# A top-32 attention with a two-expert layer on one core: third replacements, low parts and products moved between engines, row sends and check passes re-ordered

## The chip, the cores and the metric

The kernel runs on one core of a Trainium2 chip. The core's engines are TensorE (PE, with its weight loads as PEld), VectorE (DVE), ScalarE (ACT), GpSimd (POOL) and SyncE (SP), which issues DMAs. The metric is device time in microseconds (us), the median of several runs of the same program.

## The reference, cut to what matters

Every query keeps only its 32 largest scores. The attention's output is then the input of a layer of eight experts, of which each token uses two.

```python
# attention: B, H, S, D = 4, 8, 576, 64; top_k = 32
scores = scale * np.matmul(q, k.transpose(0, 1, 3, 2))
kth = np.partition(scores, -top_k, axis=-1)[..., -top_k:-top_k + 1]
scores = np.where(scores >= kth, scores, -1000000000.0)
attn = softmax(scores)
x = np.matmul(attn, v)            # 2304 rows of 512
# experts: E, F = 8, 1024
noisy = x @ w_gate + np.log1p(np.exp(x @ w_noise)) * noise
top2, top2_w = the two largest of noisy, softmax over the two
out[mask] += top2_w[mask, k, None] * (np.maximum(x[mask] @ w1[e], 0.0) @ w2[e])
```

## The kernel before, in words

The attention is cut into 144 tiles of 128 query rows, 36 for each of the four batches, `attend(j)` and `finish(j)`. For one tile the PE makes scores (L577 in batch 0, L581 later), ACT copies one half of them out (`s`, L589), and DVE folds the two halves into `cat` (maxima, then minima, L612). DVE then takes four rounds of eight maxima (L616); between rounds it overwrites the eight it has found (`drop8`, MATCH_REPLACE8, L621, over 208, 240 and 288 columns). The third replacement can be done instead by a sign on ACT (`side`, L627) and a product on GpSimd (`drop`, L630); `DROPS` gives, for each batch, in how many tenths of the tiles that is so. ACT makes the exponentials `es` (L644), a mask `mk` is made of the 32nd value, either on DVE (`mask`, L648) or as a sign on ACT (L682, after a small `below`, L678; `SIGNS` gives the tenths), and `es` is multiplied by the mask (`weigh`, L693). PE turns the product (L708, L712), ACT copies it (L716, L720), and PE multiplies by the values (L761, L768, L770).

In batches 1 to 3 the scores are made of rounded operands. ACT rounds keys and queries (`hi`, L515), and two subtractions, `low_k` (L519) and `low_q` (L522), give what the rounding left out. Each of them can go to GpSimd or to DVE.

When a batch's 36 tiles are done, `gate` and `route` choose the experts, and ten indirect DMAs from GpSimd (`scatter`, L1044, each with a small memset, L1043) send the batch's rows into per-expert buffers `xg` in DRAM. The experts run in three groups. Group 0 takes rows of batch 0 in plain fp32 (L1229, L1239, L1274) and needs the sends of batch 0; group 1 needs those up to batch 2; group 2 those of all four. Groups 1 and 2 split the weights into a rounded part (`wh`, ACT, L1112) and a rest (`wl`, L1116, on GpSimd or DVE), and multiply three times (L1200 to L1202 upward, L1282 to L1284 downward). Between them ACT and DVE split each hidden tile into `hh` (L1206) and `hl` (L1210), and each input tile into `xh` (L1170) and `xl` (L1173).

The order of all this is written by a planner, `Plan.order`, at build time: every piece has an engine, an assumed duration, dependencies and a priority, and each engine's list is then fixed. A piece with an `alt` may go to a second engine; a number (`LOWK`, `WEIGHS`, `BIAS`, `NORM`, `BELOW`, `LOWS`) shifts that choice in each batch. On the chip every engine works down its own list in that order and waits where an operand is not there. Where PE has nothing to do ahead of group 0, the planner puts in `filler` multiplies of a dummy tile (L542), in a number that `FILL` and `KEEP` set.

At the end the kernel checks that its shortcuts held (`flags`, L1006 to L1020, all on DVE, reading `over`, `under`, `left` and `apart`); if a flag is set, a slow general path follows.

## Time and profile before

| what | us |
|---|---|
| median of 3 runs | 998.77 |
| lowest and highest of them | 997.01, 1000.16 |
| the profiled execution's own time | 1007.95 |
| its span, first to last instruction | 1006.2 |

The profile is of one execution, so stretches of it are read against 1007.95 us, not against the median. Windows are counted from the span's start. By the trace batch 0's attention runs to about 150 us, group 0 from 192 to 522 us, group 1 from 520 us, the last tile's product is turned at 730 us, and from about 786 us on only group 2 is left; the last multiply of group 2 ends at 989 us. Busy shares of PE count the whole length of each multiply, and multiplies overlap. The granted clock is TensorE's, as a share of its upper level; its two levels are 1.2 and 2.4 GHz.

### The profile page before, as it was taken

What the parts mean: (1) busy time and instruction counts of PE and PEld (TensorE: products, weight loads), DVE (VectorE), ACT (ScalarE), POOL (GpSimd) and SP (SyncE); (2) the same over time, 40 slices, a digit from 0 to 9 for tenths busy, and PEclk for the clock granted to TensorE, in tenths of its full rate; (3) what the DMA queues carried; (4) which work ended last, traced back from release to release, by engine and by line L of the source; (5) the groups of instructions that cost most, each with busy time, mean ns of one, the idle gap of its engine ahead of it and who ended that gap; (6) DMA issues with size and microseconds to landing.
All of it is one profiled execution on the core that took longest, in us unless ns stands there. A gap on an engine that the chain in (4) does not pass through costs nothing.

```text
span 1006.2 us, 18439 instructions
## 1 busy us (share of the span) xinstructions
PE 940.1 (93%) x6160; PEld 788.6 (78%) x6176; DVE 695.3 (69%) x2190; ACT 680.0 (68%) x1533; POOL 742.4 (74%) x926
## 2 busy tenths in 40 slices
PE   9999998899999899999699999899978999999993
PEld 4777776787887677888489988799867888999892
DVE  6999998799999799999783578877784222222220
ACT  5888885688987478887476668577635555555550
POOL 4676677355657666677689889687858899999991
PEclk9999999799998999999999999999979999999997
DMA  9477222157366664566667677354556877776741
GB/s 281 162 259 258 49 70 93 28 155 214 125 175 175 234 172 113 154 188 149 217 231 220 168 199 191 96 159 137 137 158 206 245 215 232 233 226 211 230 126 25
DMA packets 109385, 173.92 MB, mean 173 GB/s; under 512 B 7648, under 2 KB 60896, under 8 KB 109280
## 3 DMA queue, kind: packets, MB, share of 16 engines
q1 hardware_dynamic: 100576, 152.42, 48.8%
q0 software_dynamic: 8704, 20.22, 9.7%
q8 instruction: 51, 0.84, 0.3%
q14 instruction: 54, 0.44, 0.1%
HBM read 136.34 MB, written 36.27 MB: 172 GB/s over the span
## 4 chain that ended last, share of the span: by engine, by line
PE 61%; DVE 11%; POOL 10%; ACT 7%; issue 5%; DMA 2%; another core or an unknown queue 1%; SPq 0%; POOLq 0%; DVEq 0%; ACTq 0%
PE bank L768 7%; PE hps L1200 4%; POOL wl L1116 4%; PE hps L1202 4%; PE hps L1201 4%; PE pp L708 4%; PE bk L577 4%; PE bk L581 4%; PE bk L1274 3%; PE bk L1284 3%; PE bk L1282 3%; DVE t L616 3%; PE bk L1283 3%; PE hps L1229 3%; PE hps L542 3%
## 5 line engine op out<-in xcount | busy, mean ns | idle before, releaser
L1116 POOL TENSOR_TENSOR wl<-wr,wh 128x1024 fp32r<-128x1024 f32 x118 | 292.6, 2717 | 26.6 <-ACT wh L1112 14.0
L616 DVE MAX8 t<-cat 128x8 f32<-128x288 f32 (+3 forms) x576 | 268.1, 490 | 9.4 <-POOL cat L630 6.7
L693 POOL TENSOR_TENSOR es<-es,mk 128x576 f32<-128x576 f32 x140 | 187.2, 1341 | 94.2 <-ACT mk L682 74.9
L1112 ACT ACTIVATE wh<-wr 128x1024 fp32r<-128x1024 f32 x128 | 133.7, 1056 | 51.1 <-PE bk L1284 25.4
L1210 DVE SCALAR_TENSOR_TENSOR hl<-hps,hh 128x256 fp32r<-128x256 f32 x128 | 53.8, 421 | 155.6 <-ACT hh L1206 152.8
L621 DVE MATCH_REPLACE8 cat<-t,cat 128x208 f32<-128x208 f32 (+2 forms) x408 | 159.9, 394 | 0.0
L1200 PE MATMUL hps<-xh,wh 128*128 128x256 f32 x512 | 149.9, 293 | 2.2 <-DVE hl L1210 2.2
L612 DVE TENSOR_TENSOR cat<-bk,s 128x288 f32<-128x288 f32 x288 | 125.5, 444 | 33.7 <-ACT s L589 33.5
L1202 PE MATMUL hps<-xh,wl 128*128 128x256 f32 x512 | 145.9, 285 | 0.5 <-POOL wl L1116 0.5
L1201 PE MATMUL hps<-xl,wh 128*128 128x256 f32 x512 | 145.8, 285 | 0.0
L768 PEld LDWEIGHTS bank<-vt,pt 128*128 128x128 f32 x1024 | 124.1, 196 | 15.1 <-ACT p L720 10.4
L768 PE MATMUL bank<-vt,pt 128*128 128x65 f32 x1024 | 126.3, 278 | 7.1 <-ACT p L720 7.0
L589 ACT ACTIVATE s<-bk 128x288 f32<-128x288 f32 x288 | 111.5, 416 | 31.8 <-PE bk L581 19.4
L644 ACT ACTIVATE es<-s,nb 128x576 f32<-128x576 f32 x144 | 111.7, 777 | 4.6 <-POOL nb L638 2.6
L716 ACT ACTIVATE pt<-pp 128x512 f32<-128x512 f32 x144 | 86.3, 599 | 33.8 <-PE pp L708 27.2
L1200 PEld LDWEIGHTS hps<-xh,wh 128*128 128x128 f32 x512 | 98.5, 192 | 4.6 <-DVE hl L1210 2.5
L1201 PEld LDWEIGHTS hps<-xl,wh 128*128 128x128 f32 x512 | 98.5, 192 | 2.0
L1202 PEld LDWEIGHTS hps<-xh,wl 128*128 128x128 f32 x512 | 98.3, 192 | 0.7 <-POOL wl L1116 0.7
L1206 ACT ACTIVATE hh<-hps 128x256 fp32r<-128x256 f32 x128 | 48.8, 381 | 70.6 <-PE hps L1202 66.2
L708 PE MATMUL pp<-ident,es 128*128 128x128 f32 x576 | 89.5, 278 | 7.1 <-POOL es L693 4.0
L682 ACT ACTIVATE mk<-s,under 128x576 bf16<-128x576 f32 x107 | 83.0, 780 | 16.4 <-POOL under L678 11.8
L581 PE MATMUL bk<-hi 128*128 128x288 f32 x240 | 90.0, 384 | 3.0 <-DVE cat L612 1.6
(155 smaller groups left out, 2048.0 us busy)
## 6 DMA issues: line engine op xcount, KB each, us to landing
wr<-in_w_dram SPq DMA_DIRECT2D x192, 512.0 KB, 4.7
raw<-in_qk_dram SPq DMA_DIRECT2D x48, 320.0 KB, 8.7
xg<-xs SPq DMA_DIRECT2D x16, 528.0 KB, 8.6
xs<-xg SPq DMA_DIRECT2D x16, 528.0 KB
vt<-in_v_dram SPq DMA_DIRECT2D x32, 195.0 KB, 6.3
out_dram<-xs SPq DMA_DIRECT2D x1, 5120.0 KB
hi<-in_qk_dram SPq DMA_DIRECT2D x8, 320.0 KB, 4.7
xg<-xs SPq DMA_DIRECT2D x8, 264.0 KB
```

What stands on the lines that cost most here:

```text
L581: nc.tensor.matmul(sp, lhs(n), rhs, start=(k == 0), stop=(k == 2 * len(heads) - 1))
L612: nc.vector.tensor_tensor(o, t["sp", 1], t["s"][:, :HS], op=op)
L616: return lambda: nc.vector.max(t["t8"][:, r], t["cat"] if r == 3 else t["cat"][:, slice(*TAKE[r])])
L621: nc.vector.match_replace(g, t["t8"][:, r], g, NEG)
L693: ENG[eng].tensor_tensor(t["e"], t["e"], t["mk"], op=OP.mult)
L708: nc.tensor.transpose(pp[:, c], t["e"][:, k0 + c * 128:k0 + (c + 1) * 128], ident)
L768: nc.tensor.matmul(accs[:, i + k], x["pt"][:, c], vt[n][:, c], start=(k + c == 0), stop=False, skip_group_check=True)
L1112: nc.scalar.activation(WS[n][0][:, i], W[n][:, i], AF.Copy)
L1116: return lambda eng: ENG[eng].tensor_tensor(WS[n][1][:, i], W[n][:, i], WS[n][0][:, i].bitcast(F32), op=OP.subtract)
L1200: nc.tensor.matmul(ps[:, :NN], ah, xh, start=(c == 0), stop=False)
L1201: nc.tensor.matmul(ps[:, :NN], ah, xl, start=False, stop=False)
L1202: nc.tensor.matmul(ps[:, :NN], al, xh, start=False, stop=(c == 3))
```

## The change

- `DROPS` for batches 1 and 2 goes from 0 and 1 to 4 and 3 tenths: 14 and 7 more third replacements go from DVE to ACT and GpSimd.
- `SIGNS` for batch 2 goes from 6 to 10 tenths: its 14 masks on DVE become signs on ACT.
- `low_k` and `low_q` of batches 1 and 2 lose their second engine and go to GpSimd; batch 3 keeps the choice, with another number. In a list sorted by tile, DVE's low parts go from 20 to 7.
- `weigh` loses its second engine: all 144 are on GpSimd, where 4 were on DVE.
- The sends get a priority of their own (`SENDS`), later by 30, 120, 10 and 0 than the routing of their batch.
- The flags become five reductions over all batches and five small sums, in place of 20 rounds of three instructions.
- `BIAS`, `NORM`, `KEEP` and `GLAG` get other numbers; 212 filler multiplies stand in PE's list where 182 stood.

```diff
-SIGNS = (10, 10, 6, 4)
-WEIGHS = (1500, 1600, 2300, 1900)
-BIAS = (400, 300, 800, -1100)
+SIGNS = (10, 10, 10, 4)
+BIAS = (100, 300, 800, -1100)
 BELOW = (1300, -2500, 2200, 2600)
-LOWK = (2300, 400, 500, 1300)
-NORM = (3000, 1900, 1400, 1100)
+LOWK = (2300, 400, 500, 700)
+NORM = (3300, 1900, 1400, 1100)
-FILL, KEEP = 1.1, 0.4
+FILL, KEEP = 1.1, 0.6
-DROPS = (6, 0, 1, 0)
+DROPS = (6, 4, 3, 0)
-GLAG = 1
+GLAG = 2
+SENDS = (30, 120, 10, 0)
...
-        y = add("POOL", 1545, low_k, [x], alt=("DVE", 736, LOWK[b]), lock=True)
+        y = add("POOL", 1545, low_k, [x], alt=("DVE", 736, LOWK[b]) if b == B - 1 else None, lock=True)
...
-        w = add("POOL", 1240, weigh, [mk, x2], alt=("DVE", 669, WEIGHS[b]), lock=True)
+        w = add("POOL", 1240, weigh, [mk, x2], lock=True)
...
-            for x, c, op in ((over[:, q, 0], 0.0, OP.is_gt), (over[:, q, 1], 0.0, OP.is_gt), (over[:, q, 2], 0.0, OP.is_gt),
-                             (under[:, q], -2.0 ** -100, OP.is_gt), (left[:, p], HS - 15.0, OP.not_equal) if p else (None,) * 3,
-                             (apart[:, p], 0.0, OP.is_le) if p else (None,) * 3):
-                nc.vector.tensor_scalar(fl[:, :n], x, c, None, op0=op)
-                nc.vector.tensor_reduce(fr, fl[:, :n], axis=AX.X, op=OP.add)
-                nc.vector.tensor_tensor(bad[:, 0:1], bad[:, 0:1], fr, op=OP.add)
+            red = lambda k, x, op: lambda: V.tensor_reduce(fr[:, k:k + 1], x, axis=AX.XYZW if len(x.shape) > 2 else AX.X, op=op)
+            def sums():
+                for k, c, op in ((0, 0.0, OP.is_gt), (1, -2.0 ** -100, OP.is_gt), (2, HS - 15.0, OP.not_equal),
+                                 (3, HS - 15.0, OP.not_equal), (4, 0.0, OP.is_le)):
+                    V.scalar_tensor_tensor(bad[:, 0:1], fr[:, k:k + 1], c, bad[:, 0:1], op0=op, op1=OP.add)
+            fs = [add("DVE", 60 + n / .96, red(k, x, op), notes, prio=10 ** 9) for k, n, x, op in (
+                (0, 432, over.rearrange("p j k -> p (j k)"), OP.max), (1, 144, under, OP.max), (2, 40, left, OP.max),
+                (3, 40, left, OP.min), (4, 40, apart, OP.min))]
...
-                scat.append(add("POOL", 1280, scatter(t, k), [x, g, AVN["tok", b]] + [(s, True) for s in scat[-1:]] + FILLS, move=750, lat=700))
+                scat.append(add("POOL", 1280, scatter(t, k), [x, g, AVN["tok", b]] + [(s, True) for s in scat[-1:]] + FILLS,
+                                prio=pl.prio + SENDS[b], move=750, lat=700))
```

VectorE's list after the last tile, before the change: the first flag rounds, which follow two evictions of group 1 (`xl`, `hl`); `flg`, `fr` and `bad` are the flags' own tiles.

```order
L1173 TENSOR_TENSOR xl<-hps,xh 128x256
L1210 SCALAR_TENSOR_TENSOR hl<-hps,hh 128x256
L1018 TENSOR_SCALAR flg<-over 128x36
L1019 TENSOR_REDUCE fr<-flg 128x1
L1020 TENSOR_TENSOR bad<-bad,fr 128x1
```

The same place in VectorE's list with the change:

```order
L1173 TENSOR_TENSOR xl<-hps,xh 128x256
L1210 SCALAR_TENSOR_TENSOR hl<-hps,hh 128x256
L1010 TENSOR_REDUCE fr<-over 128x1
L1010 TENSOR_REDUCE fr<-under 128x1
L1010 TENSOR_REDUCE fr<-left 128x1 x2
L1173 TENSOR_TENSOR xl<-hps,xh 128x256
L1010 TENSOR_REDUCE fr<-apart 128x1
L1015 SCALAR_TENSOR_TENSOR bad<-fr,bad 128x1 x5
L1210 SCALAR_TENSOR_TENSOR hl<-hps,hh 128x256
L796 RECIPROCAL rs<-rs 128x4
```

The flags stand where they stood, after the same two evictions and ahead of the last attention `rs`, but they are 10 instructions, where 60 stood (in three runs, with `xl`, `hl` and `rs` between the runs).

GpSimd's list at the sends of batch 1, before the change (`es` the product with the mask, `over` a note for the flags):

```order
L693 TENSOR_TENSOR es<-es,mk 128x576
L1043 MEMSET spacer 1x1
L1044 DMA xg<-xr,si 40960x528
L1043 MEMSET spacer 1x1
L1044 DMA xg<-xr,si 40960x528
```

GpSimd's list at the first two sends of batch 1 with the change:

```order
L1043 MEMSET spacer 1x1
L1044 DMA xg<-xr,si 40960x528
L694 TENSOR_TENSOR es<-es,mk 128x576
L697 TENSOR_TENSOR over<-t_4587 128x3
L694 TENSOR_TENSOR es<-es,mk 128x576
L697 TENSOR_TENSOR over<-t_4650 128x3
L679 TENSOR_SCALAR under<-t_4701 128x1
L639 TENSOR_SCALAR nb<-t_4820 128x1
L1043 MEMSET spacer 1x1
L1044 DMA xg<-xr,si 40960x528
```

Before, all ten sends followed each other after the 74th product on GpSimd; now the first five have products, notes and small pieces between them, from the 78th product on, and the last five follow each other after the 82nd. The sends of batches 0, 2 and 3 still stand in one row of ten, after the 40th, 113th and 144th product.

GpSimd's list right after the ten sends of batch 0, before the change (`xr` normalises an attention output):

```order
L1044 DMA xg<-xr,si 40960x528
L803 TENSOR_TENSOR xr<-ac,rs 128x4x64
L696 TENSOR_TENSOR over<-t_2170 128x3
L696 TENSOR_TENSOR over<-t_2248 128x3
L696 TENSOR_TENSOR over<-t_2387 128x3
L638 TENSOR_SCALAR nb<-t_2541 128x1
```

And with the change:

```order
L1044 DMA xg<-xr,si 40960x528
L804 TENSOR_TENSOR xr<-ac,rs 128x4x64
L694 TENSOR_TENSOR es<-es,mk 128x576
L697 TENSOR_TENSOR over<-t_2137 128x3
L694 TENSOR_TENSOR es<-es,mk 128x576
L697 TENSOR_TENSOR over<-t_2218 128x3
L694 TENSOR_TENSOR es<-es,mk 128x576
L697 TENSOR_TENSOR over<-t_2258 128x3
```

Three products that VectorE made while GpSimd was sending now wait in GpSimd's list behind the ten sends. In PE's list 67 fillers in one row stand ahead of the turn of tile 41 in their place, and group 0's first multiply comes after the turn of tile 44, where it came after that of tile 46.

## Rows read from the trace of the kernel before

**Rows 1.** The page's part 1, whole span: busy us, share, instructions of each engine.

```profile
PE 940.1 (93%) x6160; PEld 788.6 (78%) x6176; DVE 695.3 (69%) x2190; ACT 680.0 (68%) x1533; POOL 742.4 (74%) x926
```

**Rows 2.** Busy time by stretch: length, PE, PEld, DVE, ACT, POOL (x), clock, DMA.

```profile
175.00:200.00 25.00, 20.52 (x110) 17.35 (x112) 16.53 (x59) 14.50 (x37) 8.57 (x20) 0.80 0.13 33
200.00:300.00 100.00, 98.53 (x692) 83.02 (x691) 97.15 (x345) 88.52 (x215) 57.85 (x87) 1.00 0.59 168
...
325.00:350.00 25.00, 20.19 (x92) 14.17 (x91) 19.82 (x66) 10.46 (x32) 16.56 (x30) 0.89 0.65 225
350.00:475.00 125.00, 119.76 (x842) 101.56 (x841) 121.15 (x391) 100.86 (x256) 84.05 (x143) 1.00 0.58 152
...
725.00:750.00 25.00, 18.98 (x119) 17.02 (x118) 21.36 (x72) 10.44 (x22) 16.22 (x14) 0.87 0.46 128
750.00:775.00 25.00, 21.35 (x138) 18.34 (x138) 11.70 (x34) 9.45 (x17) 19.81 (x34) 0.92 0.64 224
775.00:975.00 200.00, 198.64 (x1283) 178.74 (x1284) 43.51 (x102) 113.42 (x188) 191.05 (x121) 1.00 0.75 219
```

**Rows 3.** VectorE in order of time, 727 to 748 us: start, length, line, what [idle].

```profile
727.74 0.75 DVE L1018 TENSOR_SCALAR flg<-over 128x36 f32<-128x36 f32 x1
...
729.78 2.18 DVE L1020 TENSOR_TENSOR bad<-bad,fr 128x1 f32<-128x1 f32 x1
...
741.31 3.56 DVE L1020 TENSOR_TENSOR bad<-bad,fr 128x1 f32<-128x1 f32 x1
...
747.65 0.24 DVE L881 TENSOR_TENSOR lgs<-lgs,bank 128x80 f32<-128x80 f32 x1 [0.27 <-issue]
```

**Rows 4.** GpSimd in order of time, the same stretch.

```profile
729.55 4.71 POOL L1116 TENSOR_TENSOR wl<-wr,wh 128x1024 fp32r<-128x1024 f32 x2 [0.94 <-POOL over L696]
```

**Rows 5.** TensorE in order of time, the same stretch: its two long waits.

```profile
735.65 0.44 PE L1166 MATMUL hps<-ident,xs 128*128 128x128 f32 x2 [1.73 <-DVE xl L1173]
...
748.28 0.80 PE L1284 MATMUL bk<-wh,hl 128*128 128x512 f32 x1 [4.29 <-DVE hl L1210]
```

**Rows 6.** VectorE's instructions by line and form, 140 to 297 us (batch 1).

```profile
L621 DVE MATCH_REPLACE8 cat<-t,cat 128x288 f32<-128x288 f32 x35 | 15.5, 442 | 0.0
...
L522 DVE TENSOR_TENSOR hi<-raw,hi 64x640 fp32r<-64x640 f32 x7 | 6.4, 917 | 0.2
...
L519 DVE TENSOR_TENSOR kl<-raw,hi 128x640 fp32r<-128x640 f32 x3 | 2.5, 819 | 0.3 <-ACT hi L515 0.3
```

**Rows 7.** The same view, 297 to 456 us (batch 2).

```profile
L648 DVE TENSOR_SCALAR mk<-s,t 128x576 bf16<-128x576 f32 x14 | 9.3, 662 | 0.0
```

**Rows 8.** Groups of instructions by line, whole span: busy us, mean ns | idle before.

```profile
L616 DVE MAX8 t<-cat 128x8 f32<-128x288 f32 (+3 forms) x576 | 268.1, 490 | 9.4 <-POOL cat L630 6.7
...
L682 ACT ACTIVATE mk<-s,under 128x576 bf16<-128x576 f32 x107 | 83.0, 780 | 16.4 <-POOL under L678 11.8 <-DVE under L678 3.1 <-POOL spacer L1301 1.4
...
L519 POOL TENSOR_TENSOR kl<-raw,hi 128x640 fp32r<-128x640 f32 x17 | 26.4, 1553 | 5.3 <-ACT hi L515 5.1
...
L630 POOL TENSOR_TENSOR cat<-cat,sg 128x288 f32<-128x288 f32 x24 | 19.2, 799 | 8.4 <-ACT sg L627 8.4
...
L627 ACT ACTIVATE sg<-cat,t 128x288 f32<-128x288 f32 x24 | 12.9, 536 | 0.0
```

**Rows 9.** VectorE's flag reductions by line and form, whole span.

```profile
L1019 DVE TENSOR_REDUCE fr<-flg 128x1 f32<-128x36 f32 x16 | 3.1, 191 | 0.6
```

**Rows 10.** GpSimd in order of time: first and last of batch 1's ten sends.

```profile
327.26 1.11 POOL L1044 DMA_INDIRECT xg<-xr,si  x1
...
338.88 1.08 POOL L1044 DMA_INDIRECT xg<-xr,si  x1 [0.24 <-issue]
```

**Rows 11.** TensorE in order of time, during those sends: its longest wait.

```profile
337.78 0.69 PE L1239 MATMUL hps<-ident,hl 128*128 128x128 f32 x2 [3.03 <-issue]
```

**Rows 12.** TensorE in order of time, after batch 0's sends (163.41 to 176.08 us).

```profile
179.41 3.68 PE L768 MATMUL bank<-vt,pt 128*128 128x65 f32 x16 [5.42 <-ACT p L720]
```

**Rows 13.** VectorE in order of time, the same place.

```profile
180.06 0.76 DVE L693 TENSOR_TENSOR es<-es,mk 128x576 f32<-128x576 f32 x1 [5.26 <-ACT mk L682]
```

More of the change, by code (lines that the diff above doesn't have):

```diff
@@ L527, in qkv @@
         hh = pl.take("hi", 4, x)
-        y = add("POOL", 1545, low_k, [x], alt=("DVE", 736, LOWK[b]), lock=True)
+        y = add("POOL", 1545, low_k, [x], alt=("DVE", 736, LOWK[b]) if b == B - 1 else None, lock=True)
         kk = pl.take("kl", 4, y)
-        z = add("POOL", 1625, low_q, [x], alt=("DVE", 850, LOWK[b]), lock=True)
+        z = add("POOL", 1625, low_q, [x], alt=("DVE", 850, LOWK[b]) if b == B - 1 else None, lock=True)
         pl.give(r, y, z)
@@ L1004, in check, with flags @@
                 V.tensor_tensor(bad[:n, 0:1], bad[:n, 0:1], st["c0"][:n], op=OP.add)
[L1006 to L1020 removed]
+        def flags():
+            fr = R.tile([128, 5], F32, name="fr")
+            red = lambda k, x, op: lambda: V.tensor_reduce(fr[:, k:k + 1], x, axis=AX.XYZW if len(x.shape) > 2 else AX.X, op=op)
[3 more added lines that the diff above has]
+                    V.scalar_tensor_tensor(bad[:, 0:1], fr[:, k:k + 1], c, bad[:, 0:1], op0=op, op1=OP.add)
+            notes = [T[j]["note"] for j in range(36 * B)]
+            fs = [add("DVE", 60 + n / .96, red(k, x, op), notes, prio=10 ** 9) for k, n, x, op in (
+                (0, 432, over.rearrange("p j k -> p (j k)"), OP.max), (1, 144, under, OP.max), (2, 40, left, OP.max),
+                (3, 40, left, OP.min), (4, 40, apart, OP.min))]
+            add("DVE", 600, sums, fs, prio=10 ** 9)
         x0 = add("ACT", 130, ex, [AVN["lgn", b]])
@@ L1058, in route @@
         if b == B - 1:
-            for i in range(B):
-                add("DVE", 2590, lambda i=i: flags(i), [T[j]["note"] for j in range(36 * B)], prio=10 ** 9)
+            flags()
         pl.give(pr, x, y, ck, g)
```

17 lines of the change are left out of this document (4 added, 13 removed).

## The prediction

> **What bounds the kernel now.** I read the busy shares of the whole span first, then the same by stretch, then who waits for whom at the dips. Over the whole span PE is busy 93% and no other engine over 74% [rows 1], so the work of PE has to be laid end to end, and time can be won only where PE waits, runs at the lower clock, or runs fillers. The stretches say where that is [rows 2]. From 775 to 975 us, with group 2 alone, PE is busy 198.64 of 200 us at full clock: nothing to win, and nothing in the change touches it. From 200 to 300 us (batch 1 with group 0) PE is busy 98.53 of 100 and DVE 97.15: both full, with ACT at 88.52 close behind. From 350 to 475 us (batch 2) DVE is busy 121.15 of 125 us and PE 119.76. The losses that can be seen stand at the joints between batches: 20.52 of 25 us at clock 0.80 (175 to 200), 20.19 at 0.89 (325 to 350), 18.98 at 0.87 and 21.35 at 0.92 (725 to 775). Each joint is the place of a batch's ten sends, and the last one also that of the flags.
>
> **The change, part by part.** The sum is made against the profiled execution's 1007.95 us, and carried to the median by their ratio, 998.77/1007.95 = 0.991.
>
> *Flags.* They hold DVE from 727.74 us to the start of `lgs` at 747.65 [rows 3], 19.9 us, of which about 1.2 us are evictions in between. Three of the small `bad` sums are long, of which two are shown, 2.18 and 3.56 us; the first ends when the first of GpSimd's two `wl` products that began at 729.55 has run its half of 4.71 us [rows 4]. In this time PE waits 1.73 us for `xl` and 4.29 us for `hl` [rows 5], and `lgs`, on which the last batch's routing and sends hang, stands behind them too. The clock of the two stretches lacks 25 x 0.13 + 25 x 0.08 = 5.3 us [rows 2]. After the change: a reduction over 36 columns took 0.19 us [rows 9], so 432 columns take at most twelve times that, 2.3 us, and at least as long as a replacement over 288, 0.44 us [rows 6]; four shorter ones some 0.2 to 0.8 us each, five sums of about 0.2 us. That is 2.3 to 6.5 us, plus up to two waits for a `wl` of 2.4 us. So DVE gives back 7 to 16 of 18.7 us. PE's part is at most 6.0 + 5.3 = 11.3 us. I take 7, since behind `hl` PE next meets `wl` products that GpSimd makes late during its own sends; ends 3 and 11.
>
> *Batch 1.* DVE loses 14 replacements of 0.442 us and ten low parts, 7 x 0.917 + 3 x 0.819 [rows 6]: 6.2 + 8.9 = 15.1 us of 157. ACT gains 14 signs of 0.536 us [rows 8], 7.5 us, which takes it from 88.5% to about 93%. GpSimd gains 14 x 0.799 + 10 x 1.553 [rows 8] = 26.7 us, from 58% to about 75%. DVE is thus free, but what is late next stands close by: ACT at 93% against DVE's 97% leaves 4% of 157, 6 us, and PE at 98.5% leaves 1.5%, 2.4 us. Against it: a replacement that leaves DVE has to come back, and DVE waited 6.7 us for GpSimd's `cat` over 24 of them [rows 8], 0.28 us each, so up to 3.9 us for 14. I take a gain of 2; ends 6 gained and 3 lost. Nearest is PE's row, since PE has to do its work whatever DVE does.
>
> *Batch 2.* DVE loses 14 masks, 9.3 us [rows 7], and 7 x 0.44 us. ACT gains 14 x 0.780 + 7 x 0.536 = 14.7 us of 159 [rows 8], from 81% to 90%. PE's idle share is 4.2% [rows 2], 6.7 us of 159. DVE was the fullest engine here and ACT has more room than in batch 1; I take 4, ends 7 gained and 3 lost by the same coming back.
>
> The Trainium skill, Perfetto Trace Analysis, section Identifying the Most-Contended Engine, says that matmul busy time is a poor measure of PE's headroom, and that the busy share of weight loads is better. By it PE has more room than I grant: the loads are busy 83.0% and 81.2% in these two stretches against 89.4% in the last one [rows 2], which would be 7 and 11 us per 100 and 125 us. The mix of multiplies differs (group 0's are long for each load), so I don't use it for the sum; it is a rival below.
>
> *Sends of batch 1.* The ten hold GpSimd from 327.26 to 339.96 us [rows 10], and masks, products and notes wait behind them. PE waits 3.03 us there [rows 11]; the stretch lacks 4.8 us of PE and 25 x 0.11 = 2.8 us of clock [rows 2]. With products between the first five, tiles go on reaching PE. The last five still follow each other, 1.28 us each. And why ACT was released late in the wait of rows 11 ("issue") the trace doesn't say, so it may come back. I take 3, ends 7.6 gained and 3 lost.
>
> *Sends of batch 0.* Here it costs. Three products that DVE made in 0.76 us [rows 13] while GpSimd was sending now wait behind 12.7 us of sends, and PE has two tiles fewer behind it when group 0 starts. A tile takes 157/35 = 4.5 us in batch 1 (one third replacement each [rows 6]), of which PE's part is less than half. On the other side PE and DVE stood still for 5.42 and 5.26 us there anyhow [rows 12, 13], and the clock lacked 25 x 0.20 = 5 us after it [rows 2]; 67 fillers in a row now keep PE at work. I take 3 us lost, ends 5 gained and 8 lost. Fillers cost nothing by themselves: group 0 can't start before its rows are there.
>
> *The rest*: batch 2's sends one product later, `GLAG`, `BIAS`, `NORM`, batch 3's low parts: work that other work covers, 0, with 3 either way.
>
> Sum: -7 - 2 - 4 - 3 + 3 = -13, so 1007.95 goes to about 995, and the median to 986.
>
> **The rivals.**
>
> *Only the flags count.* PE at 98.5% is the bound of batch 1, the joints move and don't shrink, batch 2 gives nothing. For it: PE's busy row. Against it: the 5 us of visible idle of batch 2. -7 + 3 = -4, so about 995.
>
> *GpSimd's list becomes the bound at the joints; slower.* GpSimd takes 27 us more in batch 1 and never reorders. At the joint of batch 0 three products of 1.3 us, notes, low parts and replacements queue up behind 12.7 us of sends. It decides if the queue outlasts the lead of DVE, four `es` buffers, 4 x 4.5 = 18 us: then DVE stands still, each joint costs 5 to 8 us instead of less, and batches 1 and 2 give nothing: -7 + 8 + 3 + 5 = +9, so about 1008. Against it: GpSimd was busy only 58% and 67% in these batches, so that it makes up the queue within two or three tiles.
>
> *More DVE instructions held up by GpSimd.* The `bad` sum of 2.18 us [rows 3] lasted until a `wl` ended [rows 4]; an instruction of this size takes 0.2 us otherwise. If DVE's remaining instructions are held like this for GpSimd's 27 more us, at worst a third of it comes back on DVE in each of batches 1 and 2, and takes their gain away, about -7 - 3 + 3 + 2 = -5, so 994. The Trainium skill, GPSIMD Engine Reference, section Key points, says that GpSimd shares its memory interfaces with VectorE and contends with instructions that have two operands in SBUF or run in a 2-port mode, which speaks against this change. By the same rows the change also takes such instructions away from DVE (low parts, masks), so I hold it for small.
>
> *More room on PE.* If the 15 us that DVE loses in batch 1 and the 12 us in batch 2 shorten their stretches by 8 and 8, -7 - 8 - 8 - 3 + 3 = -23, so about 976. This is also what the rule on weight loads in Perfetto Trace Analysis (the Trainium skill) would lead to. ACT at 93% speaks against it.
>
> **How the numbers follow.** Within 0.3% means 995.8 to 1001.8 us, about what a measurement of this kernel can tell from no change. The forecast (986) has 0.57; only the flags (995) 0.16; GpSimd's list (1008) 0.12; held up (994) 0.06; more room (976) 0.09. Faster: 0.53 of the forecast's 0.57, half of the 0.16, 0.05 and 0.09 make 0.75. Within 0.3%: 0.04 + 0.08 + 0.01 and a little of the slow case, 0.14. Slower: 0.11. The ends of the terms, taken together as unlikely to fall on one side, give 13 us either way, 973 to 999; I carry the upper end to 1001 for part of the second rival's short cases and leave its full price out.
>
> **What would show it.** Flags: on DVE from the first reduction over `over` to the end of the last `bad` sum under 10 us, no PE wait over 2 us between the last turn and `lgs`, and a clock of 1.00 there. Batch 1 and 2: DVE's share under 92%, ACT's over 90%, tiles 44 to 108 passed in less time than now. Sends of batch 1: no PE wait of 3 us amid them. Batch 0: PE's fillers at full clock through the sends, group 0's first multiply 0 to 5 us later than 192 us. I'd be wrong if DVE's share falls and the tiles come no faster, or if PE waits for `es` after sends for longer than 6 us at two joints.

## The result, and the profile after

The changed kernel ran at 1009.5 us (median of four runs, 1007.54 to 1013.93), the kernel before beside it at 997.9: a ratio of 1.0122, with a 95% interval of 1.0092 to 1.0152. It is slower, where 986 us was forecast. In a later session of ten runs the same kernel stood at 1.0038 (0.9992 to 1.0083) of the kernel before, with single runs from 983.89 to 1002.44 us; how that goes together is what the experiments found out. The ratios leave out single runs over 1.5% above the fastest of the same kernel, which here are part of the runs with the fall described below: with all ten runs of this later session the medians stand at 1.0089.

The profiled execution took 1009.41 us, with a span of 1007.6. The first part of its page, beside [rows 1]:

```profile
PE 957.5 (95%) x6191; PEld 795.2 (79%) x6206; DVE 655.2 (65%) x2071; ACT 701.3 (70%) x1597; POOL 777.5 (77%) x988
```

TensorE is busier than before (95% against 93%) and the kernel is slower. At the lower clock a multiply is busy for longer (from 105 to 125 us, below, 63 multiplies fill 19.66 us where 140 filled 19.77), and a filler is busy too; this share says nothing of work done. The granted clock in 40 slices of the span, first of the kernel before, then of the changed one:

```profile
PEclk9999999799998999999999999999979999999997
```

```profile
PEclk9998579999999999999989999999999999999997
```

The dips at 175 us and at the last joint are gone, and a new and deeper one stands at 75 to 150 us, in batch 0, where the prediction expected nothing. The stretches that answer to [rows 2] (length, PE, PEld, DVE, ACT, POOL, clock, DMA):

```profile
175.00:200.00 25.00, 24.27 (x152) 14.76 (x154) 17.41 (x71) 12.06 (x29) 21.27 (x42) 1.00 0.28 99
200.00:300.00 100.00, 96.77 (x667) 81.26 (x668) 85.14 (x299) 89.27 (x228) 72.91 (x121) 0.98 0.49 138
325.00:350.00 25.00, 22.19 (x148) 17.85 (x147) 23.95 (x81) 19.29 (x48) 19.15 (x40) 0.93 0.31 105
350.00:475.00 125.00, 119.19 (x827) 100.25 (x825) 110.46 (x373) 109.03 (x279) 100.02 (x174) 1.00 0.56 168
725.00:750.00 25.00, 24.35 (x176) 22.29 (x175) 17.99 (x43) 15.20 (x33) 19.36 (x17) 1.00 0.45 149
750.00:775.00 25.00, 21.70 (x150) 18.63 (x149) 16.94 (x37) 9.96 (x19) 21.48 (x34) 1.00 0.69 215
775.00:975.00 200.00, 197.96 (x1279) 178.31 (x1279) 44.30 (x103) 113.18 (x188) 190.34 (x124) 1.00 0.76 223
```

VectorE is as free as forecast (85 of 100 us where it was 97, 110 of 125 where it was 121), and the tiles come no faster: from tile 44's turn to tile 72's it took 117.1 us (117.3 before), from tile 80's to tile 108's 119.6 us (109.9 before).

Busy time being no measure, the stretches of the two kernels, and of two of the experiments, are compared by the time that TensorE did *not* spend on real multiplies. For each form of multiply (its tiles and its shape) a usual short distance to the next one at full clock is its price. The prices add up to 820 us in every kernel, fillers left out; a stretch less the prices of its multiplies is what was lost there, to waits, fillers and the lower clock:

```
us lost         before  changed  e4: flags alone  e18: changed + gate fillers
0 to 75           28.3     28.2             27.5                        29.0
75 to 150         22.2     33.7             22.3                        25.5
150 to 225        28.4     32.4             24.7                        27.5
225 to 300         5.4      9.4              8.2                         9.8
300 to 350        13.7     10.3              7.1                         9.4
350 to 475        12.5     13.8             15.1                        13.6
475 to 525        13.4     11.6              7.3                         4.4
525 to 650        14.2      7.4             13.4                         6.9
650 to 725         4.7      5.3              5.5                         6.5
725 to 800        18.9     10.2              8.7                         9.6
800 to end        24.4     24.9             24.0                        23.7
sum              185.9    187.3            164.1                       165.9
```

The columns are one execution each. With prices by shape alone (the median distance) the changed kernel loses 11.9 us more than before from 75 to 150 us and 9.1 less from 725 to 800, so these two rows hold; the other differences between these two columns move by up to 4 us, and those of 4 us or less are weak evidence.

**The fall of the clock in batch 0.** The same stretches of before and of the changed kernel, one after the other (columns as above):

```profile
90.00:95.00 5.00, 5.00 (x36) 4.06 (x35) 4.85 (x18) 3.75 (x12) 3.30 (x6) 1.00 1.03 393
95.00:100.00 5.00, 5.00 (x31) 3.81 (x30) 4.21 (x11) 5.00 (x12) 3.14 (x9) 1.00 1.04 321
105.00:125.00 20.00, 19.77 (x140) 14.50 (x142) 18.33 (x63) 18.35 (x50) 12.63 (x26) 1.00 0.23 54
```

```profile
90.00:95.00 5.00, 5.00 (x32) 3.81 (x31) 4.58 (x15) 3.82 (x11) 2.76 (x7) 1.00 1.05 408
95.00:100.00 5.00, 5.00 (x16) 3.24 (x13) 4.67 (x17) 4.43 (x12) 3.60 (x8) 0.54 1.05 398
105.00:125.00 20.00, 19.66 (x63) 13.01 (x63) 10.65 (x35) 9.49 (x22) 7.30 (x14) 0.50 0.00 1
```

From 95 to 136 us TensorE is granted 1.2 GHz (0.50); it is busy nearly all the time and from 105 to 125 us does 63 multiplies where it did 140, and VectorE, ACT and GpSimd do about half as much beside it. Ahead of the fall it is busy 5.00 of 5 us too, by the profile's count of each multiply's whole length. What differs is which multiplies these are. TensorE in order of time (start, length, line, what), before:

```profile
88.96 1.19 PE L865 MATMUL bank<-wg,xt 128*128 128x16 f32 x10
90.00 0.64 PE L708 MATMUL pp<-ident,es 128*128 128x128 f32 x4
90.57 1.72 PE L577 MATMUL bk<-hi 64*128 64x288 f32 x6
92.22 2.00 PE L768 MATMUL bank<-vt,pt 128*128 128x65 f32 x16
```

and the changed kernel:

```profile
88.17 2.00 PE L769 MATMUL bank<-vt,pt 128*128 128x65 f32 x16
...
90.72 0.27 PE L855 MATMUL bank<-ident,xr 128*128 128x128 f32 x1
90.92 1.23 PE L578 MATMUL bk<-hi 64*128 64x288 f32 x4
92.08 1.29 PE L866 MATMUL bank<-wg,xt 128*128 128x16 f32 x10
93.30 1.23 PE L578 MATMUL bk<-hi 64*128 64x288 f32 x4
```

`GLAG` moved the gate of batch 0's second quarter (a turn, then ten multiplies of 16 columns) by one tile: it stood ahead of the sixteen multiplies by the values and stands behind them now, 2 to 3 us ahead of the fall. The number moves the gates of the first three quarters of every batch, not of this one alone.

**The joint after batch 0.** GpSimd in order of time, from the first send to the first replacement that it makes for VectorE:

```profile
185.57 1.22 POOL L1044 DMA_INDIRECT xg<-xr,si  x1 [0.19 <-POOL spacer L1043]
...
197.37 0.92 POOL L1044 DMA_INDIRECT xg<-xr,si  x1 [0.24 <-issue]
198.35 0.61 POOL L804 TENSOR_TENSOR xr<-ac,rs 128x256 f32<-128x256 f32 x1
198.93 1.26 POOL L694 TENSOR_TENSOR es<-es,mk 128x576 f32<-128x576 f32 x1
200.31 1.27 POOL L694 TENSOR_TENSOR es<-es,mk 128x576 f32<-128x576 f32 x1
201.70 1.26 POOL L694 TENSOR_TENSOR es<-es,mk 128x576 f32<-128x576 f32 x1
203.23 0.78 POOL L631 TENSOR_TENSOR cat<-cat,sg 128x288 f32<-128x288 f32 x1
```

and VectorE, whose idle time stands in the brackets:

```profile
204.05 0.76 DVE L617 MAX8 t<-cat 128x8 f32<-128x576 f32 x1 [10.53 <-POOL cat L631]
...
211.27 0.82 DVE L613 TENSOR_TENSOR cat<-bk,s 128x288 f32<-128x288 f32 x2 [6.27 <-ACT s L590]
```

VectorE stands still for 16.8 us in two waits behind the sends and the queue that built up behind them, where [rows 13] had 5.26 us. TensorE runs fillers meanwhile (45 in one row from 189.41 us), so no long wait of TensorE tells of it.

**The flags.** VectorE from the first reduction to the last sum and to `lgs`, which answers to [rows 3], and GpSimd at the same time, to [rows 4]:

```profile
738.56 0.60 DVE L1010 TENSOR_REDUCE fr<-over 128x1 f32<-128x432 f32 x1 [0.80 <-POOL over L697]
...
740.11 4.68 DVE L1015 SCALAR_TENSOR_TENSOR bad<-fr,bad 128x1 f32<-128x1 f32 x5
...
750.92 0.23 DVE L882 TENSOR_TENSOR lgs<-lgs,bank 128x80 f32<-128x80 f32 x1
```

```profile
739.50 4.70 POOL L1116 TENSOR_TENSOR wl<-wr,wh 128x1024 fp32r<-128x1024 f32 x2 [0.97 <-POOL over L697]
```

They take 6.2 us, evictions included, where 19.9 us stood. Two of the five sums last as long as the two `wl` beside them (the longest 2.27 us, the median 0.16). The waits of TensorE from the last turn on, beside [rows 5]:

```profile
PE bk L1284 <- DVE hl L1210: 2.4, 3, 1.1
PE hps L1200 <- DVE hl L1210: 1.9, 1, 1.9
```

### The profile page after: what moved, and what is told of

The parts are those of the page before. It is cut to its first block, busy times and chain, and to the rows that moved or that the text cites. A ratio compares the mean times of both kernels' runs of the same rounds, so it can differ in the third digit from the quotient of the medians.

```text
span 1007.6 us, 18491 instructions
## 1 busy us (share of the span) xinstructions
PE 957.5 (95%) x6191; PEld 795.2 (79%) x6206; DVE 655.2 (65%) x2071; ACT 701.3 (70%) x1597; POOL 777.5 (77%) x988
## 5 line engine op out<-in xcount | busy, mean ns | idle before, releaser
L1116 POOL TENSOR_TENSOR wl<-wr,wh 128x1024 fp32r<-128x1024 f32 x117 | 289.0, 2692 | 16.0 <-ACT wh L1112 12.2
L617 DVE MAX8 t<-cat 128x8 f32<-128x208 f32 (+3 forms) x576 | 268.5, 491 | 27.9 <-POOL cat L631 24.5
L622 DVE MATCH_REPLACE8 cat<-t,cat 128x208 f32<-128x208 f32 (+2 forms) x387 | 151.2, 393 | 0.0
L769 PEld LDWEIGHTS bank<-vt,pt 128*128 128x128 f32 x1024 | 127.3, 199 | 12.1 <-ACT p L721 6.3
L683 ACT ACTIVATE mk<-s,under 128x576 bf16<-128x576 f32 x122 | 93.2, 780 | 27.3 <-POOL under L679 12.9
L709 PE MATMUL pp<-ident,es 128*128 128x128 f32 x576 | 92.8, 286 | 5.4 <-POOL es L694 4.0
L582 PE MATMUL bk<-hi 128*128 128x288 f32 x240 | 87.8, 376 | 6.7 <-DVE cat L613 3.2
```

Source lines behind the costliest of these rows:

```text
L617: return lambda: nc.vector.max(t["t8"][:, r], t["cat"] if r == 3 else t["cat"][:, slice(*TAKE[r])])
L622: nc.vector.match_replace(g, t["t8"][:, r], g, NEG)
L769: nc.tensor.matmul(accs[:, i + k], x["pt"][:, c], vt[n][:, c], start=(k + c == 0), stop=False, skip_group_check=True)
L1116: return lambda eng: ENG[eng].tensor_tensor(WS[n][1][:, i], W[n][:, i], WS[n][0][:, i].bitcast(F32), op=OP.subtract)
```

## The experiments

Each session ran the kernel before beside its own; its medians there were 995.4, 985.8, 987.5, 995.7 and 987.3 us, so ratios are what can be compared across sessions.

### The kernel before once more, and the flags alone

The kernel before, unchanged:

> The kernel before, once more, to have a second profile of it: the one at hand is of an execution of 1007.95 us, 9 us over the median, so its losses may not be those of a usual execution. If the profile at hand is typical but late by a bit everywhere, this one shows the same dips of the clock (175 to 200, 300 to 350, 500 to 525, 625 to 650, 725 to 775 us) and a mean clock of 0.97. If not, it has a mean clock of 0.98 or more, a span of 994 to 999 us and one or two of these dips are missing. In both cases the clock stays at 1.00 from 25 to 150 us, where the changed kernel is at 0.5 for 40 us.

Its median was 999.6 us (ten runs), 1.0038 (0.999 to 1.0086) of the same kernel's other runs, and single runs lay between 987.78 and 1009.21 us at a mean clock of 0.984 to 0.969. The second profile (1002.84 us) has the dips at 160 to 188, 495, 635 and 738 to 748 us again, one at 407 us that the first hasn't, and not the one at 320 to 340 us. The profile that the prediction read was thus of a late execution of a kernel whose executions differ by 2%, mostly by short falls of the clock.

The kernel before with the new flags:

```diff
-            for i in range(B):
-                add("DVE", 2590, lambda i=i: flags(i), ...)
+            flags()    # five reductions, five sums
```

> The kernel before with the new flags alone. By the prediction's term the flags are worth 7 us (3 to 11): 987 to 995 us against 998. In the profile of the changed kernel the clock after the last tile is no better by more than 5 us and the stretch from the last turn to the end has the same length (276 and 268 us), so the rival is that they are worth 0 to 3 us, 995 to 998 us: what DVE gives back is lost behind GpSimd's sends.

> The kernel before with the new flags alone, a second time, on the chip of the three that follow. The price of the flags should hold on another chip: 0.986 to 0.996 of the kernel before, and no fall of the clock between 25 and 150 us. If the first chip made it (it ran the kernel before at 995 us where two others ran it at 986 and 988), the ratio is 0.996 to 1.002.

0.9916 (0.9875 to 0.9956) in one session and 0.9932 (0.9886 to 0.9977) in another: 8.4 and 6.8 us, as forecast (7). In both sessions the kernel before took 995.4 and 995.7 us, against 985.8 to 987.5 in the other three; the alternative that the second run was to try, no gain beside a kernel before of 986 us, thus stays untried. The flags alone took 984.73 and 985.76 us. The stretch from 725 to 800 us loses 8.7 us where it lost 18.9, and the second profile of the kernel before loses as much there as the first. TensorE in the two stretches of [rows 2] with the flags alone:

```profile
725.00:750.00 25.00, 21.70 (x158) 19.24 (x157) 16.47 (x36) 10.59 (x21) 21.47 (x34) 1.00 0.68 208
750.00:775.00 25.00, 24.51 (x157) 21.43 (x157) 8.89 (x17) 16.67 (x28) 21.50 (x19) 1.00 0.77 243
```

So the flags are right in their own stretch, and the rest of the change costs more than they win. One part of the second expectation failed: its profiled execution (1006.52 us, the slowest of eleven) has the clock at half from 10.7 to 31.1 us, in batch 0 and with `GLAG` at 1. Its clock in 40 slices:

```profile
PEclk7899999899999799998989999999999999999997
```

### What brings the fall of the clock

```diff
-GLAG = 2
+GLAG = 1
```

> The changed kernel with GLAG at 1 again, so that the gate pieces of a batch's quarters stand one tile earlier, as in the kernel before. First theory (the clock of batch 0): the changed kernel is slower because its TensorE is granted 1.2 GHz from 97 to 137 us, and what sets that off is the new order of batch 0, in which only GLAG, KEEP, BIAS and NORM act. If GLAG is the cause, the fall at 97 us is gone, tile 32 is reached 15 to 20 us earlier, and the end moves by 5 to 15 us, to 995 to 1004 us. If it isn't, the fall stays and the time stays at 1009 +- 3. Rival (GpSimd's load): batches 2 and 3 are slower, and the fall of the clock in batch 0 is given back by the joint with batch 1 anyhow; then the time stays at 1009 even without the fall.

1.0116 (1.0076 to 1.0156). The fall in batch 0 is gone from the profile, and still the ratio is no better: this order has falls and waits of its own between 320 and 580 us. By the measure of the table it loses about 12 us less than the changed kernel from 75 to 150 us, and 8 to 13 more (by either price) from 350 to 475 and 6 to 7 more from 525 to 650. The first half of the theory held, the time did not follow.

```diff
-FILL, KEEP = 1.1, 0.6
+FILL, KEEP = 1.1, 0.4
```

> The changed kernel with KEEP at 0.4 again, which gives 215 fillers in place of 212, 1 to 3 of them ahead of tile 32. If the fall of the clock at 97 us hangs on these few fillers, it is gone and tile 32 is reached 15 to 20 us earlier, with a time of 995 to 1004 us. If it hangs on the order that GLAG sets, the fall stays and the time stays at 1009 +- 3.

1.0056 (0.9999 to 1.0114), and the ten runs fall into two groups: six at 991.8 to 996.9 us with a mean clock of 0.978 to 0.986, four at 1005.9 to 1010.7 with 0.966 to 0.971. The profile is of the first group and has no fall in batch 0. The medians of the groups lie 14 us apart. Its list for batch 0 has one filler more up to tile 32 (107 for 106) and two by tile 40.

The kernel before with the new flags, and all that acts in batch 0:

```diff
-BIAS = (400, 300, 800, -1100)
-NORM = (3000, 1900, 1400, 1100)
-FILL, KEEP = 1.1, 0.4
-GLAG = 1
+BIAS = (100, 300, 800, -1100)
+NORM = (3300, 1900, 1400, 1100)
+FILL, KEEP = 1.1, 0.6
+GLAG = 2
```

> The kernel before with the new flags, and besides only BIAS, NORM, KEEP and GLAG of the changed kernel, which give its order of the first 28 tiles (the same 44, 48, 61, 63, 75, 76, 84 fillers ahead of every fourth tile). If that order sets off the fall of TensorE's clock near 97 us, the profile shows it, the mean clock is 0.96 to 0.975 and the time 998 to 1005 us in all runs; with no fall, 985 +- 4 at 0.98 or more. Rival: the fall has its cause in something else (the moves reach batch 0 only from tile 28 on), and then this kernel stays at 985.

1.0199 (1.0128 to 1.0271), with the clock at half from 93 to 124 us in its profile: the fall comes with these four numbers, without any of the moves in batches 1 and 2. The median of its four runs is 1011.98 us, beside 985.84. Then the changed kernel again, and with more fillers all over batch 0:

> The changed kernel once more, on the chip of the three kernels that it is to be compared with. If the fall of the clock near 97 us belongs to its order of batch 0 on every chip, its mean clock is 0.96 to 0.972 in all runs and it stands 10 to 16 us above the next kernel (10 fillers more in batch 0); if the fall came of one chip, part of its runs show 0.98 and more.

```diff
-FILL, KEEP = 1.1, 0.6
+FILL, KEEP = 1.1, 0.0
```

> The changed kernel with KEEP at 0, which gives more fillers in batch 0: 47, 51, 64, 66, 79, 80, 88, 109 ahead of every fourth tile in place of 44, 48, 61, 63, 75, 76, 84, 104; the rest of the order is nearly the same. Clock theory: with 3 to 4 dummy multiplies more (1.1 us of work) ahead of tile 20 the clock stays at 1.00 from 25 to 150 us, all runs have a mean clock of 0.98 or more, and the time falls by 10 to 16 us against the changed kernel. Rival: the fall comes of another engine's stop (a DMA or VectorE ahead of 95 us), fillers don't help, and the two kernels agree within 4 us.

The changed kernel again: 1.0038 (0.9992 to 1.0083). Its profile has the fall at 95 to 123 us; three of ten runs have a mean clock of 0.980 to 0.985 and take 983.89 to 989.75 us, the other seven have 0.966 to 0.975 and take 994.10 to 1002.44: 13 us between the medians of the two groups. In the first session all four runs had 0.963 to 0.969; so the fall does not come in every run, as the first expectation had it. With more fillers it was 1.0344 (1.0299 to 1.0389), with the fall at 95 to 126 us still there: this expectation failed. More fillers elsewhere in batch 0 did not prevent the fall.

Then `GLAG` and `KEEP` each by itself, on top of the kernel before with the new flags:

```diff
-GLAG = 1
+GLAG = 2
```

> The kernel before with the new flags and GLAG = 2, nothing else. Theory: moving the gate pieces of a quarter one tile later is enough to bring the fall of the clock at 93 to 96 us; it shows in the profile or in part of the runs, which then have a mean clock of 0.955 to 0.972 and stand 10 to 20 us above the new flags alone. Rival: KEEP's fewer fillers are needed too; then no run falls, and the time is that of the new flags alone within 4 us.

```diff
-FILL, KEEP = 1.1, 0.4
+FILL, KEEP = 1.1, 0.6
```

> The kernel before with the new flags and KEEP = 0.6, nothing else: 44, 48, 63, 64, 75, 75, 77, 91 fillers ahead of every fourth tile in place of 45, 49, 64, 65, 76, 76, 78, 92, and the sends and gate pieces where they were. If KEEP's missing filler takes part in the fall of the clock, some runs lose it (mean clock under 0.972, 10 us or more over the others). If the gate pieces alone decide, no run falls in batch 0 and the time is that of the new flags alone, 0.986 to 0.998 of the kernel before.

`GLAG` alone: 1.0411 (1.026 to 1.0562), four runs. The profiled run (1014.05 us) has no fall in batch 0; the other three have a mean clock of 0.946 to 0.954 against its 0.966, which is what one such fall would take off, but no profile shows where they lost it. And the fall isn't all that `GLAG` costs here: the profiled run, without it, stands 28 us above the flags alone of the same session (985.76), where 10 to 20 were expected. By the measure of the table it loses 8 to 12 us more than the flags alone (e4) from 225 to 350 us, 7 to 8 more from 525 to 650 and 11 more from 725 to 800. `KEEP` alone: 0.989 (0.985 to 0.993), a median of 975.96 us with no run under a mean clock of 0.983. So `KEEP` alone brings no fall; whether it adds to the flags alone isn't shown, since the two intervals overlap and come from different sessions.

Last, the whole changed kernel, with work put beside the moved gate multiplies:

```diff
         def mm():
+            if b == 0 and c < 3:
+                filler(8)
             for t in range(NT):
                 nc.tensor.matmul(bank[:, 388 + t * 16:404 + t * 16], ...)
```

> The changed kernel, all of it, with eight dummy multiplies put ahead of the ten small gate multiplies of each of batch 0's first three quarters (5 us of TensorE's time in all, in batch 0, where VectorE is the bound). Theory: the fall at 93 to 96 us comes of the small multiplies of the second gate, which GLAG moved from 88 to 92 us; with dummy multiplies beside them it is gone, the profile shows the clock at 1.00 from 75 to 140 us, most runs have a mean clock of 0.978 or more, and the time is 0.99 to 1.003 of the kernel before. Rival: the fall isn't set off there; then most runs still fall and the time is 1.004 to 1.015.

1.0005 (0.997 to 1.004), ten runs of 984.6 to 994.11 us, all at a mean clock of 0.983 to 0.99. TensorE at the place where the clock fell, and the clock in 40 slices:

```profile
93.13 1.69 PE L543 MATMUL hps<-dummy 128*128 128x512 bf16 x7 [0.16 <-issue]
94.66 1.18 PE L868 MATMUL bank<-wg,xt 128*128 128x16 f32 x10
```

```profile
PEclk9999999999999899999999999999999999999997
```

The profile has no fall in batch 0, by their mean clock the other nine runs have none, and the kernel stands where the three runs of e9 without the fall stood (984 to 990 us beside a kernel before of 987.5). This is the strongest evidence for the place. Two things it leaves open: the changed kernel without these fillers did not run beside it, and the dummy multiplies also move the ten by 1.7 us, so that the work beside them and the shift are not told apart. Over all profiles, the clock fell between 75 and 140 us in none of the eleven with `GLAG` at 1 and in five of the eight with `GLAG` at 2 and no fillers at the gate. Earlier in batch 0 it fell with `GLAG` at 1 too, in the profile of 1006.52 us named above, so the gate is not the only place in batch 0 for such a fall. What decides in one execution and not in the next is open: e10 and e11 have the same fillers in batch 0, and one profile has the fall and the other hasn't.

### What the moves and the sends are worth

Each on top of the kernel before with the new flags, whose own ratio is 0.992:

```diff
-        w = add("POOL", 1240, weigh, [mk, x2], alt=("DVE", 669, WEIGHS[b]), lock=True)
+        w = add("POOL", 1240, weigh, [mk, x2], lock=True)
```

> The kernel before with the new flags, and besides only the products with the mask all on GpSimd (4 of 144 move). Theory (GpSimd's list at the joint): in the changed kernel VectorE stands still 10.5 and 6.3 us behind GpSimd's sends of batch 0, since the products that stood on VectorE there now wait for the sends. If the four products make it, this kernel shows two waits of VectorE of over 4 us between 165 and 215 us, and loses 3 to 8 us against the new flags alone (985 us): 988 to 993. Rival: the standstill comes of the replacements that GpSimd makes right behind the sends; then these four products change nothing, 985 +- 3.

```diff
-SIGNS = (10, 10, 6, 4)
-LOWK = (2300, 400, 500, 1300)
-DROPS = (6, 0, 1, 0)
+SIGNS = (10, 10, 10, 4)
+LOWK = (2300, 400, 500, 700)
+DROPS = (6, 4, 3, 0)
...  low_k and low_q of batches 1 and 2 on GpSimd alone
```

> The kernel before with the new flags, and besides only the moves of batches 1 and 2: SIGNS, DROPS and the low parts of keys and queries as in the changed kernel; the products keep their second engine. By the prediction's terms it gains 2 + 4 us on the new flags alone, 976 to 982 us. By the theory of GpSimd's list it is no faster, since replacements and low parts then stand behind the sends of batch 0 and VectorE waits for the first of them: a wait of VectorE for a product that GpSimd puts into cat of 4 to 10 us near 180 us, and 985 to 995 us. By a third view (the moves gain what they save on VectorE, and only the products cost), 972 to 978 us.

```diff
+SENDS = (30, 120, 10, 0)
...
+                                prio=pl.prio + SENDS[b], move=750, lat=700))
```

> The kernel before with the new flags, and besides only SENDS = (30, 120, 10, 0): the ten sends of batch 1 then stand after 74, 75, 76, 76, 77, 77, 78, 78, 79 and 79 products in place of 74, those of batches 0, 2 and 3 where they stood. By the prediction's term it gains 3 us (3 lost to 7.6 gained), 982 us; the standstill of TensorE in the sends of batch 1 is gone. Rival: what TensorE waits for there is not made up of the sends, and group 1's rows come no sooner: 985 +- 2.

```diff
-SIGNS = (10, 10, 6, 4)
+SIGNS = (10, 10, 10, 4)
```

> The kernel before with the new flags and SIGNS of batch 2 at 10 tenths, nothing else: 14 masks move from VectorE to ACT, GpSimd's list stays. By the prediction's term for batch 2 it gains 2 to 4 us on the new flags alone, with VectorE busy 8 to 9 us less between 350 and 475 us. Rival: TensorE's own work is the bound there (its time without real work is 12 to 17 us of the 125 in every kernel so far), and the time stays within 2 us.

The products: 0.9984 (0.9955 to 1.0012). The moves: 1.0149 (1.0099 to 1.02). The sends: 1.0114 (1.0053 to 1.0175). The masks of batch 2 alone: 1.0151 (1.0018 to 1.0284). None of them gains, and three of the four lose 2% or so against the flags alone. The flags alone did not run in the session of the first three; in us the products (984.29) stand level with them (984.73 and 985.76), the moves (996.95) and the sends (993.13) above. The masks did run beside them: 1004.94 against 985.76 us. They are the plainest case, since only VectorE and ACT change. The stretch of batch 2 with the flags alone:

```profile
350.00:475.00 125.00, 117.81 (x846) 99.62 (x846) 121.54 (x398) 100.59 (x256) 84.34 (x141) 1.00 0.61 159
```

and with the masks moved too:

```profile
350.00:475.00 125.00, 111.16 (x795) 93.88 (x794) 117.14 (x382) 103.96 (x253) 83.27 (x149) 0.98 0.48 132
```

VectorE is freed, by 4.4 us of the 8 to 9 expected, and TensorE does *less*: 795 multiplies in place of 846. TensorE's waits of over 0.3 us add up to 13.0 us there, where the flags alone had 6.4; half of that are short waits for GpSimd's products and ACT's copies, which this order brings at other times, and the clock falls once, from 470 us. Which of them comes first isn't settled.

Whether VectorE's standstill at the joint comes of the products or of the replacements was tried with the fillers of e10 (ratios there are no guide, since the fall of the clock comes and goes):

```diff
-        w = add("POOL", 1240, weigh, [mk, x2], lock=True)
+        w = add("POOL", 1240, weigh, [mk, x2], alt=("DVE", 669, WEIGHS[b]), lock=True)
```

> As the run with KEEP at 0, with the second engine of the products given back (4 products on VectorE, 3 of them at the joint after batch 0, so that the replacement for VectorE stands right behind the sends). Theory (GpSimd's list at the joint): VectorE's wait for that replacement falls from 10.6 us by three products and notes, 4.3 us, to about 6, and the time falls by 2 to 5 us. Rival: PE's bound hides it (it has fillers there), and the time stays within 2 us.

```diff
-DROPS = (6, 4, 3, 0)
+DROPS = (6, 0, 1, 0)
```

> As the run with KEEP at 0, with DROPS = (6, 0, 1, 0) as in the kernel before, so that no replacement for VectorE stands behind the sends of batch 0; products and low parts still do. Theory: the wait of VectorE for cat from GpSimd of 10.6 us near 195 us is gone, what is left is the wait for ACT's s of about 6 us, and batch 1's stretch from the sends to its last tile is 5 us shorter; the time falls by 2 to 6 us. Rival: the three products stop the turns just as long, VectorE stops a few us later for the want of es buffers, and the time stays within 2 us. Prediction's own view of the moves of replacements (2 + 1 us gained by them): the time rises by 3.

VectorE's waits at the joint (160 to 225 us: in all, times, longest), with the products back, and then with the replacements back:

```profile
DVE t L618 <- POOL cat L632: 10.7, 2, 9.2
DVE cat L614 <- ACT s L591: 4.8, 3, 3.8
```

```profile
DVE rs L796 <- ACT rs L792: 14.4, 1, 14.4
DVE cat L613 <- ACT s L590: 3.4, 1, 3.4
```

Both expectations failed on the standstill: it stays at 15 to 18 us and only changes its name. With the products alone moved (e5) the longest such wait is 2.6 us, with the later sends alone (e8) 0.4, with the moves alone (e6) two of 5.0 and 4.2. So none of the pieces by itself brings the standstill; that it takes several together in GpSimd's list is what remains, and was not tried. The times were 1012.0 and 1015.6 us (medians of four), beside 1019.5 for e10.

The changed kernel with both of its batch 0 numbers back:

```diff
-FILL, KEEP = 1.1, 0.6
-GLAG = 2
+FILL, KEEP = 1.1, 0.4
+GLAG = 1
```

> The changed kernel with both GLAG and KEEP of the kernel before (1 and 0.4), so that batch 0 up to tile 20 has the order and the fillers of the kernel before; flags, moves, products, sends, BIAS and NORM stay changed. Theory (GLAG's order sets off the fall): no fall of the clock between 75 and 140 us, a mean clock of 0.975 or more, and a time of 0.99 to 1.003 of the kernel before, since the flags' 8 us stand against 5 to 8 us lost behind GpSimd's sends. Rival (the moves themselves make it slower by more than the flags win): 1.005 to 1.015 with no fall in batch 0, as the run with GLAG at 1 had it.

1.0122 (0.9998 to 1.0245), four runs, and no fall in batch 0 in the profile. By the medians (1004.92 and 995.66 us) moves, products and sends stay slower than the kernel before even so, though the interval reaches down to 1; this order has falls of its own between 320 and 585 us. The theory, which expected 0.99 to 1.003, put too much on the one fall.

## Why the prediction was wrong

The miss is 23.5 us. The terms were to take the profiled 1007.95 us to 995; the profiled execution after is 1009.41, so 14.4 us are due to the terms. The other 9 are due to the step from the profile to the median, 0.991: it took the 9 us by which that execution was late for a share of every execution, while the profile of the changed kernel is no later than its median. The late execution had its own falls of the clock, and such falls don't scale.

*The rest, 0 with 3 either way: this step failed.* `GLAG`, `BIAS` and `NORM` were put down as work that other work covers. `GLAG` moved ten small multiplies on TensorE by 3 us, the clock fell, and batch 0 lost 11.5 us more than before (75 to 150 us); between runs with and without the fall lie 13 to 14 us. And the term has no one size: on top of the flags alone `GLAG` costs 28 us without that fall (e15), and in the changed kernel its going back loses elsewhere what it wins in batch 0 (e2). The prediction costed instructions by how long they last and where they wait. It didn't ask, of a piece moved on TensorE, what stands beside it. The Trainium skill, TensorE: Matmul & The Clock Gate, section HAM oscillation — how this bites in real kernels, names idle gaps of the engine as what brings such falls. The trace of this fall shows none: TensorE was busy 5.00 of 5 us ahead of it.

*Flags, -7: right.* 725 to 800 us lost 8.7 us less, the flags alone gave 8.4 and 6.8 in two sessions, and the marks set for it held: under 10 us on VectorE (6.2), no wait of TensorE over 2 us (1.9), the clock at 1.00. Two long waits for `wl` were foreseen, and two came.

*Sends of batch 0, +3 with 5 gained to 8 lost: the mechanism is there, the size is in part luck.* 150 to 225 us lost 4.0 us more. The mechanism was the one named, products behind 12.7 us of sends, and more of it than thought: VectorE stood still for 16.8 us, hidden from TensorE's waits by fillers. But e18 has the same two waits of VectorE (10.5 and 6.3 us) and loses 27.5 us there, 0.9 less than before and 2.8 more than the flags alone. Group 0's work on TensorE began 13 us later than before, not 0 to 5, since batch 0 itself ended late.

*Batch 1, -2, and batch 2, -4: not there.* 225 to 300 us lost 4.0 us more, 350 to 475 us 1.3 more. The text named the sign by which it would be wrong, VectorE's share falling and the tiles coming no faster, and that is what [rows 2] and the rows above show. ACT came to 89% and 87%, not over 90%. A full VectorE was read as the limit of batch 2; moving its 14 masks alone gained nothing (e16). What does set the pace there stays open. The rival that gave TensorE more room, after the rule on weight loads in Perfetto Trace Analysis (section Identifying the Most-Contended Engine; the Trainium skill), falls with it: the loads' share went from 83.0% to 81.3% and from 81.2% to 80.2% where the rival wanted it to rise.

*Sends of batch 1, -3: the size is there and the reason isn't.* 300 to 350 us lost 3.4 us less, but the flags alone, with the sends where they were, lose only 7.1 there, and TensorE's wait of 3.03 us is gone without any change to the sends: the 13.7 belonged to that one execution. The mark itself held (no wait of TensorE over 1.1 us amid the sends).

*What no term had:* 525 to 650 us lost 6.8 us less in the changed kernel (2.7 with prices by shape alone), and 6.5 less in e18 than in e4 (4.3). With the products alone 9.5 us are lost there, with any other part alone 12 or more; with `GLAG` back at 1 and all else changed (e2) it is 13 again, so `GLAG` has a part in it. Which others it takes was not tried.

Of the rivals, the slower one (GpSimd's list, 1008 us) came nearest to the time and was right on its mechanism at one of three joints; that its sum fits is luck, since the fall in batch 0 is not among its terms. The rival by which VectorE's instructions are held up by GpSimd's is not seen in the tiles' maxima. The group that answers to the first of [rows 8]:

```profile
L617 DVE MAX8 t<-cat 128x8 f32<-128x208 f32 (+3 forms) x576 | 268.5, 491 | 27.9 <-POOL cat L631 24.5
```

A MAX8 took 491 ns, and 490 before. What grew is the wait for `cat` ahead of it, 24.5 us over 45 replacements where it was 6.7 over 24. Of the 24.5 us, 10.53 are the one standstill behind the sends of batch 0; the other 44 waited 0.32 us each, near the 0.28 that the prediction's lower end for batch 1 was made of. The Trainium skill, GPSIMD Engine Reference, section Key points, speaks of contention of GpSimd with VectorE's instructions that have two operands in SBUF or run in a 2-port mode. Here it fits the sums of the flags beside `wl` (2.27 us where the median is 0.16); the tiles have too few such instructions left to tell (four `low_k`, 1.07 us each, where seven took 1.00).

The best version that the runs found is the kernel before with the new flags and `KEEP` at 0.6 (e17): 0.989 (0.985 to 0.993) of the kernel before, and 975.96 us beside 986.33 for the changed kernel with fillers at the gate.

## What to carry to other kernels

When a change moves even a few small multiplies on TensorE, look at what stands beside them and at the granted clock there: a fall in a stretch that waits tile by tile can cost more (13 to 14 us here) than the surest saving of the change (the flags' 7 to 8). Read a dip as something to win only where two executions have it, and carry an execution's lateness to the median as microseconds that may not come again, not as a ratio. In a kernel with a planned order, test each part by itself before adding up: of the six parts that ran alone here, two ran in a kernel faster than before (the flags, and `KEEP` on top of them).

## What was not expected of the hardware

The clock fell while TensorE had no idle time in the profile, behind a turn and ten multiplies of 16 columns, and in batch 0 it stayed down for 27 to 41 us (five profiles; 20 us in a sixth, which fell at 10.7 us behind a wait of 0.84), where falls later in the same kernels last 3 to 14 us. With eight dummy multiplies of 512 columns ahead of the ten the profile has no fall there, and ten runs have a mean clock of 0.983 or more. The same program's runs differ by 2% (985.44 to 1005.06 us in one session of the kernel before), and a run's mean clock orders them: 0.987 for the first, 0.971 for the last.
